# Chunked RWKV attention and a feed-forward layer on one core: `v` cast on GpSimd, joined masks and state sums, a second output bank, and DMA transposes from the 17th chunk on

## The chip, the cores and the metric

The kernel runs on one core of one Trainium2 chip. The time is the device time of one execution in microseconds, and lower is better. The engines carry the profile's names: PE (matrix multiplications; PEld loads its weights), DVE (VectorE), ACT (ScalarE), POOL (GpSimd), SP (SyncE, which issues the DMAs here).

## The reference

The inputs are `r`, `k`, `v`, `w` of shape (4, 8, 768, 48), that is batch, heads, time and head size, `u` of (8, 48), and the weights `w_in` (384, 2048) and `w_out` (2048, 384). In float32:

```python
for t in range(S):
    cur = einsum('bhd,bhe->bhde', u[None] * kt, vt)
    y[:, :, t] = einsum('bhd,bhde->bhe', rt, state + cur)
    state = wt[:, :, :, None] * state + einsum('bhd,bhe->bhde', kt, vt)
x = y.transpose(0, 2, 1, 3).reshape(B * S, H * D)     # 3072 x 384
h = x @ w_in
out = np.maximum(0.01 * h, h) @ w_out                 # 3072 x 384
```

## The kernel before

Time is cut into chunks of 128 steps: 6 chunks for each of the 4 batches, 24 in all, numbered from 0. The state passes from chunk to chunk inside a batch. All matrix products are in bf16.

For one chunk the **attention** goes through these steps (names of tiles as in the profile). Four loads bring `w`, `k`, `r`, `v` into one slot of the ring `in` (11 slots, which the weights use too). ACT takes the logarithm of `w` (`lw`), PE sums it over time (`cp`, with the chunk's total behind it), DVE and ACT make the two exponentials (`ci`, `er`, `ek`), and DVE multiplies them onto `r` and `k` (both halves of `rk`). PE transposes `rk` in eight blocks into a PSUM bank, DVE and ACT copy the halves out (`rkT`). PE makes the scores (banks `se`, `so`: even and odd heads), DVE multiplies them with the mask (`m`, two instructions). `vb` is `v` cast to bf16 (L323, on DVE). PE multiplies the `k` half of `rk` with `vb` (`pp`), DVE adds it to the decayed old state (`s`, two instructions on 64 partitions each), POOL decays the state for the next chunk (`sb`, two instructions, with the factor `a` from ACT). PE adds state and scores up (`yp`), DVE adds the diagonal term that POOL prepared (`ru`, `dg`, `vs`) and gets `y`; PE transposes `y` in three blocks, ACT copies it to `xT`.

The **feed-forward layer** takes each chunk from `xT`: 48 matmuls in four groups of 12 (`hp`, two banks), an activation on ACT after each group (`g`), 16 matmuls in four groups of 4 (`op`, one bank), a copy on DVE (`o`), a store by SP.

PSUM has eight banks: `hp` 2, and one each for `op`, `cp`, `se`, `so`, `yp`, `pp`. The transposes of `rk` go through `se`, those of `y` through `so`.

**What sets the order.** Nothing is recorded in the order of the code. Every step is entered into a `Plan` with an engine, a planned duration, its dependencies and a priority (ten times the chunk number for attention, 1000 and up for the matmuls of the feed-forward layer). The planner goes through time with these planned durations, gives each engine the ready step of the lowest priority number, and adds a delay `LAT` to each result. The order in which it started the steps becomes the order of the instructions of each engine, and on the chip every engine keeps that order and waits where a result isn't there. So a planned duration has no effect on the chip but through the order. Two rules hold the attention near the feed-forward layer: `LEAD` = 4 lets a chunk's logarithm wait for the first `hp` of the chunk four before, and `AHEAD` = 5 lets its loads wait for the `cp` of the chunk five before. `WEIGHTS` says before which chunk's steps, and with which priority, the eight weight loads of 0.79 MB are entered.

Of the kernel before, what the change touches and what calls it, by code (L numbers as in the profile page):

```python
# [8 lines left out]
F32 = mybir.dt.float32  # L9
# [6 lines left out]
class Plan:  # L16
# [3 lines left out]
    LAT = 0.12  # L20
# [15 lines left out]
    def order(self):  # L36
# [18 lines left out]
        while events:  # L55
# [14 lines left out]
            if self.wire[i] is None:  # L70
                done[i] = free[e] + self.LAT
            else:
                dma_free = max(dma_free, free[e]) + self.wire[i]
                done[i] = dma_free + 1.7
# [41 lines left out]
def kernel(  # L116
# [23 lines left out]
    APE = 24  # L140
    NPE = 24
# [3 lines left out]
    WEIGHTS = [(1, 4)] * 4 + [(3, 24)] * 4  # L145
# [6 lines left out]
    def ring(name, count, shape, dtype, where=None):  # L152
        return Ring([(where or pool).tile(shape, dtype, name=f"{name}{i}") for i in range(count)])
# [14 lines left out]
    er_r = ring("er", 3, [128, H, 64], F32)  # L168
# [8 lines left out]
    a_r = ring("a", 3, [128, NP], F32)  # L177
    sx_r = ring("s", 3, [128, NP, D], F32)
# [5 lines left out]
    dram = ctx.enter_context(tc.tile_pool(name="dram", bufs=1, space=bass.MemoryType.DRAM))  # L184
    ad_r = ring("ad", 4, [1, H * 64], F32, dram)
    hp_r = ring("hp", 2, [128, 512], F32, psum)
    op_r = ring("op", 1, [128, DM], F32, psum)
    cp_r = ring("cp", 1, [128, 512], F32, psum)
    se_r = ring("se", 1, [128, NP, 128], F32, psum)
    so_r = ring("so", 1, [128, NP, 128], F32, psum)  # L190
    yp_r = ring("yp", 1, [128, H, D], F32, psum)
    pp_r = ring("pp", 1, [128, NP, 2, D], F32, psum)

    with tc.manual_schedule():
# [3 lines left out]
        for t in sb_r.tiles:  # L198
            nc.gpsimd.memset(t[:], 0.0)
        for t in er_r.tiles:  # L200
            nc.gpsimd.memset(t[:], 1.0)
# [31 lines left out]
        def dve(n, src=60):  # L233
            return (src + n) / 960.0 + 0.03

        def act(n, src=180):
            return (src + n) / 1200.0
# [7 lines left out]
        def weight_steps(q, which, pri):  # L245
# [16 lines left out]
            for half, eng in ((0, "DVE"), (1, "ACT")):  # L262
# [13 lines left out]
                d = dve(384) if eng == "DVE" else act(768, 224)  # L276
# [6 lines left out]
        for n in range(NCH):  # L283
# [19 lines left out]
            if n == 0:  # L303
# [18 lines left out]
                "DVE", dve(DM // 2),  # L322
                lambda vb=vb, vn=vn: nc.vector.tensor_copy(out=vb.t[:], in_=vn.t),  # L323
# [4 lines left out]

            a_pe = n < APE

            def cum(cp=cp, lw=lw, tot=(not first and a_pe)):
# [3 lines left out]
                if tot:  # L335
# [6 lines left out]
            s_cum = step("PE", 0.35 if not first and a_pe else 0.17, cum, P0, reads=[lw], writes=[cp], deps=[s_ln])  # L342
# [12 lines left out]
                    out=er.t[:, :, 0:D], in_=cp.t[:, 0:DM].rearrange("p (h d) -> p h d", h=H), func=AF.Exp),  # L355
                P0, reads=[cp], writes=[er], deps=[s_cum],
# [9 lines left out]
                "DVE", dve(DM),  # L366
                lambda rk=rk, rn=rn, er=er: nc.vector.tensor_tensor(  # L367
                    out=rk.t[:, 0, :, 0:D], in0=rn.t, in1=er.t[:, :, 0:D], op=ALU.mult),
# [3 lines left out]
                "DVE", dve(DM),  # L372
# [6 lines left out]
            if n < NPE:  # L379
                tr = se_r.take()  # L380
                trv = tr.t[:].bitcast(BF16).rearrange("p a (b t) -> p (a b) t", b=2)

                def tpose(rk=rk, trv=trv):
                    for g in range(2 * NP):
                        nc.tensor.transpose(  # L385
                            trv[:, g, :],
                            rk.t[:, g // NP, 2 * (g % NP) : 2 * (g % NP) + 2, :].rearrange("p h d -> p (h d)"),
                            ident[:])
                s_tr = step("PE", 0.6, tpose, P0, reads=[rk], writes=[tr], deps=[s_r, s_k])
                s_t1 = step(  # L390
                    "DVE", dve(512, 120),
                    lambda trv=trv, rkT=rkT: nc.vector.tensor_copy(out=rkT.t[:, 0:NP, :], in_=trv[:, 0:NP, :]),  # L392
                    P0, reads=[tr], writes=[rkT], deps=[s_tr])
                s_t2 = step(
                    "ACT", act(512),
                    lambda trv=trv, rkT=rkT: nc.scalar.copy(out=rkT.t[:, NP:, :], in_=trv[:, NP:, :]),  # L396
                    P0, reads=[tr], writes=[rkT], deps=[s_tr])
                s_T = [s_t1, s_t2]
            else:
# [4 lines left out]
                    P0, reads=[rk], writes=[rkT], deps=[s_r, s_k], wire=1.0)]  # L404
# [13 lines left out]
                "DVE", dve(DM),  # L418
# [3 lines left out]
                "POOL", 1.05,  # L422
# [5 lines left out]
            se, so, yp = se_r.take(), so_r.take(), yp_r.take()  # L428
            sb = None
            if not first:  # L430
                a_in = a_r.take()
                if a_pe:
                    s_adep = step(
                        "ACT", act(NP),
                        lambda a_in=a_in, cp=cp: nc.scalar.activation(  # L435
                            out=a_in.t[:], in_=cp.t[:, DM : DM + NP], func=AF.Exp),
                        P0 + 1, reads=[cp], writes=[a_in], deps=[s_cum])
                else:

                    ad = ad_r.take()  # L440
                    s_row = step(
                        "SP", 0.45,
                        lambda ad=ad, er=er: nc.sync.dma_start(
                            out=ad.t[:], in_=er.t[0:1].rearrange("o h d -> o (h d)")),
                        P0 + 1, reads=[er], writes=[ad], deps=[s_er], wire=0.02)
                    s_sp = step(
                        "SP", 0.45,
                        lambda ad=ad, a_in=a_in: nc.sync.dma_start(
# [236 lines left out]
```

## Time and profile before

| | |
|---|---|
| Time, median of 2 runs | 222.24 us (221.99 to 222.48) |
| The profiled execution | 222.69 us, its span 220.8 us |
| Granted TensorE clock, mean | 0.969 |
| Busy: PE, DVE, ACT, POOL | 186.3, 155.6, 118.7, 98.6 us |
| Moved by DMA | 30.47 MB, 64.7% of 16 engines' span |

The span is what the profile covers; the time of the same execution is 1.9 us longer. A group's row reads: line, engine, operation, output and inputs, shapes, count | busy us in all, mean ns of one | idle time of the engine just before them, and what ended it. In the timeline and in the chain the first number is the start and the second the length, both in us.

### The profile page before, as it was taken

Reading aid. Unit: us, or ns where it says so; the run is one execution under the profiler, and the core shown is the slowest. Engines: PE = TensorE matmul, PEld = TensorE weight load, DVE = VectorE, ACT = ScalarE, POOL = GpSimd, SP = SyncE. Lnnn points to the kernel's source line nnn. Section 1 sums busy time; section 2 is a strip of 40 time slices with the busy share of each in tenths; the row PEclk is TensorE's granted clock in tenths of the full one; section 3 lists DMA queues with packets and bytes.
Section 4 is the critical chain, followed back from the end, with each engine's and each line's share of the span. In section 5 each row is a group of like instructions: output and inputs, shape, how many; then the busy total and the mean of one; then the engine's idle time right before and its main releaser. Section 6 shows DMA issues by size and latency. Waiting matters only on the chain.

```text
span 220.8 us, 6043 instructions
## 1 busy us (share of the span) xinstructions
PE 186.3 (84%) x2448; PEld 144.2 (65%) x2448; DVE 155.6 (70%) x299; ACT 118.7 (54%) x245; POOL 98.6 (45%) x125
## 2 busy tenths in 40 slices
PE   0446679887979998949899999999999999999983
PEld 0246457665667776736686778777777777788861
DVE  6653995589999999996878876977967565620021
ACT  3347367565566655615465547656555655545420
POOL 6312740687663965666787573474412211200000
PEclk9999559999999999988999999999999999999999
DMA  7999999999999999939089267846010110001101
GB/s 130 318 355 184 297 355 165 179 193 189 200 185 216 188 210 201 200 76 181 18 162 177 61 122 147 174 98 128 36 39 2 37 39 36 3 36 39 39 36 71
DMA packets 107179, 30.47 MB, mean 138 GB/s; under 512 B 100368, under 2 KB 105616, under 8 KB 107152
## 3 DMA queue, kind: packets, MB, share of 16 engines
q1 hardware_dynamic: 107152, 30.09, 64.7%
q8 instruction: 19, 0.31, 0.6%
q14 instruction: 8, 0.07, 0.1%
HBM read 25.36 MB, written 4.72 MB: 136 GB/s over the span
## 4 chain that ended last, share of the span: by engine, by line
PE 49%; DVE 23%; DMA 8%; ACT 7%; issue 7%; SPq 2%; POOL 2%; DVEq 0%; ACTq 0%; POOLq 0%
PE hp L579 19%; PE op L631 18%; DVE rk L373 4%; DVE ci L347 3%; DMA in<-in_moe_w_in_dram 3%; DVE m L494 3%; PE se L385 3%; DVE s L510 3%; PE se L471 3%; DMA in<-in_w_dram 2%; DVE y L537 2%; ACT er L354 2%; DMA in<-in_r_dram 2%; DVE vb L323 2%; PE so L547 2%
## 5 line engine op out<-in xcount | busy, mean ns | idle before, releaser
L579 PE MATMUL hp<-xT,w_in_b 128*128 128x128 bf16 x1152 | 81.0, 225 | 0.8 <-ACT xT L553 0.8
L613 ACT ACTIVATE g<-hp 128x512 bf16<-128x512 f32 x96 | 57.4, 598 | 39.4 <-PE hp L579 38.5
L631 PE MATMUL op<-w_out_b,g 128*128 128x384 bf16 x384 | 77.8, 329 | 0.6 <-DVE o L642 0.6
L579 PEld LDWEIGHTS <-w_in_b 128*128 128x128 bf16 x1152 | 72.5, 101 | 7.5 <-issue 1.2
L631 PEld LDWEIGHTS <-g 128*128 128x128 bf16 x384 | 33.1, 98 | 16.5 <-issue 1.8
L462 POOL TENSOR_TENSOR sb<-s,a 64x192 bf16<-64x192 f32 x40 | 25.6, 639 | 28.8 <-ACT a L435 24.9
L411 POOL TENSOR_TENSOR ru<-in,ub 128x384 f32<-128x384 f32 x24 | 24.7, 1033 | 25.0 <-DMA in<-in_r_dram 21.1
L423 POOL TENSOR_TENSOR vs<-in,dg 128x384 f32<-128x384 f32 x24 | 20.0, 834 | 35.2 <-DVE dg L419 11.4
L642 DVE COPY o<-op 128x384 f32<-128x384 f32 x24 | 13.3, 555 | 23.2 <-PE op L631 22.8
L415 POOL TENSOR_TENSOR ru<-ru,in 128x384 f32<-128x384 f32 x24 | 25.7, 1074 | 1.5
L385 PE MATMUL se<-ident,rk 128*128 128x128 bf16 x192 | 18.3, 230 | 7.8 <-DVE rk L367 3.9
L396 ACT COPY rkT<-se 128x512 bf16<-128x512 bf16 x24 | 14.0, 585 | 19.2 <-DVE rkT L392 12.8
L494 DVE TENSOR_TENSOR m<-se,maskb 128x512 bf16<-128x512 f32 x24 | 16.5, 689 | 6.8 <-ACT g L613 3.7
L385 PEld LDWEIGHTS <-rk 128*128 128x128 bf16 x192 | 12.5, 101 | 12.7 <-DVE rk L373 6.0
L367 DVE TENSOR_TENSOR rk<-in,er 128x384 bf16<-128x384 f32 x24 | 18.2, 759 | 2.3 <-ACT er L354 2.1
L347 DVE TENSOR_TENSOR ci<-cp,lw 128x384 f32<-128x384 f32 x24 | 13.3, 553 | 8.3 <-PE cp L337 5.1
L373 DVE TENSOR_TENSOR rk<-in,ek 128x384 bf16<-128x384 f32 x24 | 18.0, 750 | 1.2 <-ACT ek L360 1.1
L537 DVE TENSOR_TENSOR y<-yp,vs 128x384 bf16<-128x384 f32 x24 | 13.2, 550 | 7.8 <-PE yp L526 7.7
L354 ACT ACTIVATE er<-cp 128x384 f32<-128x384 f32 x24 | 11.8, 491 | 10.6 <-DVE ci L347 6.1
L547 PE MATMUL so<-ident,y 128*128 128x128 bf16 x72 | 8.5, 231 | 9.5 <-DVE y L537 9.2
L494 DVE TENSOR_TENSOR m<-so,maskb 128x512 bf16<-128x512 f32 x24 | 16.3, 680 | 0.0
L360 ACT ACTIVATE ek<-ci 128x384 f32<-128x384 f32 x24 | 12.5, 520 | 5.8 <-DVE ci L347 5.8
(42 smaller groups left out, 193.1 us busy)
## 6 DMA issues: line engine op xcount, KB each, us to landing
in<-in_w_dram SPq DMA_DIRECT2D x24, 192.0 KB, 4.2
in<-in_k_dram SPq DMA_DIRECT2D x24, 192.0 KB, 4.1
in<-in_r_dram SPq DMA_DIRECT2D x24, 192.0 KB, 4.4
in<-in_v_dram SPq DMA_DIRECT2D x24, 192.0 KB, 4.4
out_dram<-o SPq DMA_DIRECT2D x24, 192.0 KB, 2.0
in<-in_moe_w_in_dram SPq DMA_DIRECT2D x4, 768.0 KB, 8.2
in<-in_moe_w_out_dram SPq DMA_DIRECT2D x4, 768.0 KB, 8.7
ub<-in_u_dram SPq DMA_DIRECT2D x1, 192.0 KB, 5.0
```

The lines of the kernel that those rows point to most:

```text
L347: lambda cp=cp, ci=ci, lw=lw: nc.vector.tensor_tensor(out=ci.t[:], in0=cp.t[:, 0:DM].rearrange("p (h d) -> p h d", h=H), in1=lw.t[:, :, 0: ...
L367: lambda rk=rk, rn=rn, er=er: nc.vector.tensor_tensor(out=rk.t[:, 0, :, 0:D], in0=rn.t, in1=er.t[:, :, 0:D], op=ALU.mult),
L373: lambda rk=rk, kn=kn, ek=ek: nc.vector.tensor_tensor(out=rk.t[:, 1, :, 0:D], in0=kn.t, in1=ek.t[:], op=ALU.mult),
L385: nc.tensor.transpose(trv[:, g, :], rk.t[:, g // NP, 2 * (g % NP) : 2 * (g % NP) + 2, :].rearrange("p h d -> p (h d)"), ident[:])
L411: lambda ru=ru, rn=rn: nc.gpsimd.tensor_tensor(out=ru.t[:], in0=rn.t, in1=ubv, op=ALU.mult),
L415: lambda ru=ru, kn=kn: nc.gpsimd.tensor_tensor(out=ru.t[:], in0=ru.t[:], in1=kn.t, op=ALU.mult),
L423: lambda vs=vs, vn=vn, dg=dg: nc.gpsimd.tensor_tensor(out=vs.t[:], in0=vn.t, in1=dg.t[:].unsqueeze(2).to_broadcast([128, H, D]), op=ALU.mult),
L462: lambda sb=sb, s_in=s_in, a_in=a_in, q0=q0, half=half: nc.gpsimd.tensor_tensor(out=sb.t[q0 : q0 + 64, :, half, :], in0=s_in.t[q0 : q0 + 6 ...
L494: lambda m=m, sc=sc, par=par: nc.vector.tensor_tensor(out=m.t[:, par, :, :], in0=sc.t[:], in1=maskb[:].unsqueeze(1).to_broadcast([128, NP, ...
L579: nc.tensor.matmul(hp.t[:, a * N : (a + 1) * N], lhsT=w_in_b[:, t, (j + a) * 128 : (j + a + 1) * 128], rhs=xT[:, t, c0 : c0 + N], start=(a ...
L613: lambda hp=hp, g=g, j=j, J=J, N=N: nc.scalar.activation(out=g.t[:, j : j + J, 0:N], in_=hp.t[:, 0 : J * N].rearrange("p (a n) -> p a n", ...
L631: nc.tensor.matmul(op.t[:], lhsT=g.t[:, j, off : off + 128], rhs=w_out_b[:, j, :], start=(j == 0), stop=(j == NJ - 1))
```

## The change

- `v` is cast to bf16 by POOL instead of DVE.
- The scores of even and odd heads share one tile `sc` of two banks, and one mask instruction of 1,024 columns takes the place of two of 512. The transposes of `rk` go through `sc`, in two steps: those of the `r` half no longer stand in one step with those of the `k` half.
- The state is kept with both heads' columns on all 128 partitions; `a` holds zeros where they don't belong together (written by two activations on 64 partitions each). So one state sum on DVE and one decay on POOL take the place of two each.
- `pp`, `yp` and the transposes of `y` share one bank `yp`; the freed bank is a second `op`.
- From chunk 16 on (`NPE` = 16 instead of 24) `rk` and `y` are transposed by one DMA each, issued by SP, with no copy by DVE or ACT.
- The planner's numbers: `LAT` is 0.28 for PE and 0.07 for the others instead of 0.12 for all, many planned durations differ, and `WEIGHTS` enters the loads of `w_in` before chunk 2 with priority 14 (before chunk 1 with 4), those of `w_out` before chunk 4 with 34 (before chunk 3 with 24).

```diff
-    LAT = 0.12
+    LAT = {"PE": 0.28, "DVE": 0.07, "ACT": 0.07, "POOL": 0.07, "SP": 0.07}
...
-    NPE = 24
+    NPE = 16
-    WEIGHTS = [(1, 4)] * 4 + [(3, 24)] * 4
+    WEIGHTS = [(2, 14)] * 4 + [(4, 34)] * 4
...
-    op_r = ring("op", 1, [128, DM], F32, psum)
+    op_r = ring("op", 2, [128, DM], F32, psum)
-    se_r = ring("se", 1, [128, NP, 128], F32, psum)
-    so_r = ring("so", 1, [128, NP, 128], F32, psum)
-    yp_r = ring("yp", 1, [128, H, D], F32, psum)
-    pp_r = ring("pp", 1, [128, NP, 2, D], F32, psum)
+    yp_r = pp_r = ring("yp", 1, [128, 512], F32, psum)
+    sc_r = ring("sc", 1, [128, 2, NP, 128], F32, psum)
...
             s_vb = step(
-                "DVE", dve(DM // 2),
-                lambda vb=vb, vn=vn: nc.vector.tensor_copy(out=vb.t[:], in_=vn.t),
+                "POOL", 0.8,
+                lambda vb=vb, vn=vn: nc.gpsimd.tensor_copy(out=vb.t[:], in_=vn.t),
...
-                    P0, reads=[rk], writes=[rkT], deps=[s_r, s_k], wire=1.0)]
+                    P0, reads=[rk], writes=[rkT], deps=[s_r, s_k], wire=1.75)]
...
-                for half in range(2):
-                    q0 = 64 * half
-                    s_sb.append(step(
-                        "POOL", 0.5,
-                        lambda sb=sb, s_in=s_in, a_in=a_in, q0=q0, half=half: nc.gpsimd.tensor_tensor(
-                            out=sb.t[q0 : q0 + 64, :, half, :], in0=s_in.t[q0 : q0 + 64],
-                            in1=a_in.t[q0 : q0 + 64].unsqueeze(2).to_broadcast([64, NP, D]), op=ALU.mult),
+                s_sb = [step(
+                    "POOL", 1.05,
+                    lambda sb=sb, s_in=s_in, a_in=a_in: nc.gpsimd.tensor_tensor(
+                        out=sb.t[:].rearrange("p g a d -> p (g a) d"),
+                        in0=s_in.t[:].rearrange("p g a d -> p (g a) d"),
+                        in1=a_in.t[:].rearrange("p g a -> p (g a)").unsqueeze(2).to_broadcast([128, H, D]),
+                        op=ALU.mult),
...
-            for par, sc in enumerate((se, so)):
-                s_m.append(step(
-                    "DVE", dve(NP * 128, 120),
+            s_m = [step(
+                "DVE", 1.2,
+                lambda m=m, sc=sc: nc.vector.tensor_tensor(
+                    out=m.t[:].rearrange("p a g t -> p (a g) t"),
+                    in0=sc.t[:].rearrange("p a g t -> p (a g) t"),
+                    in1=maskb[:].unsqueeze(1).to_broadcast([128, H, 128]), op=ALU.mult),
...
+                def state(sx=sx, pp=pp, sb=sb):
...
+                        nc.vector.tensor_tensor(out=sx.t[:], in0=pp.t[:, 0:DM].rearrange("p (g a d) -> p g a d", g=NP, a=2), in1=sb.t[:], op=ALU.add)
...
             if n < NPE:
-                tr = so_r.take()
-                trv = tr.t[:].bitcast(BF16).rearrange("p a (b t) -> p (a b) t", b=2)
+                trv = yp.t[:].bitcast(BF16).rearrange("p (g t) -> p g t", t=128)
```

Three places show what this does to the order. The first is SP's queue in the start, from the last load of chunk 2 (slot `in_75`) on. Before, `w_out` (slots 76 to 79) comes next, then the loads of chunk 4 (slot 70) and chunk 3 (slot 69) in turn:

```order
L297 DMA in_75<-in_v_dram 128x8x48
L255 DMA in_76<-in_moe_w_out_dram 128x4x384
L255 DMA in_77<-in_moe_w_out_dram 128x4x384
L255 DMA in_78<-in_moe_w_out_dram 128x4x384
L255 DMA in_79<-in_moe_w_out_dram 128x4x384
L297 DMA in_70<-in_w_dram 128x8x48
L297 DMA in_70<-in_k_dram 128x8x48
L297 DMA in_69<-in_w_dram 128x8x48
L297 DMA in_69<-in_k_dram 128x8x48
L297 DMA in_69<-in_r_dram 128x8x48
L297 DMA in_69<-in_v_dram 128x8x48
L297 DMA in_70<-in_r_dram 128x8x48
```

And now the same place, where chunk 3 has slot 76, `w_out` has 77 to 79 and 69, and chunk 4 has slot 70:

```order
L290 DMA in_75<-in_v_dram 128x8x48
L290 DMA in_76<-in_w_dram 128x8x48
L290 DMA in_76<-in_k_dram 128x8x48
L290 DMA in_76<-in_r_dram 128x8x48
L290 DMA in_76<-in_v_dram 128x8x48
L248 DMA in_77<-in_moe_w_out_dram 128x4x384
L248 DMA in_78<-in_moe_w_out_dram 128x4x384
L248 DMA in_79<-in_moe_w_out_dram 128x4x384
L248 DMA in_69<-in_moe_w_out_dram 128x4x384
L290 DMA in_70<-in_w_dram 128x8x48
```

Chunk 3's loads moved ahead of `w_out`. In the same way chunk 1's loads now stand ahead of `w_in`, behind which they stood before.

The second place is DVE in the middle, one chunk's round from one `rk` of `k` to the next. Before:

```order
L373 TENSOR_TENSOR rk_91<-in_75,ek_89 128x8x48
L323 CAST vb_101<-in_75 128x384
L419 TENSOR_REDUCE dg_106<-ru_105 128x8
L347 TENSOR_TENSOR ci_83<-cp_146,lw_81 128x384
L537 TENSOR_TENSOR y_125<-yp_149,vs_109 128x384
L392 COPY rkT_95<-se_147 128x512
L510 TENSOR_TENSOR s_121<-pp_150,sb_123 64x192 x2
L367 TENSOR_TENSOR rk_92<-in_76,er_86 128x8x48
L373 TENSOR_TENSOR rk_92<-in_76,ek_88 128x8x48
L323 CAST vb_102<-in_76 128x384
L494 TENSOR_TENSOR m_113<-se_147,maskb 128x512
L642 COPY o_134<-op_145 128x384
```

And now, from one `rk` of `k` to the next:

```order
L366 TENSOR_TENSOR rk_91<-in_75,ek_89 128x8x48
L616 COPY o_134<-op_140 128x384
L512 TENSOR_TENSOR y_125<-yp_142,vs_109 128x384
L387 COPY rkT_95<-sc_143 128x512
L340 TENSOR_TENSOR ci_83<-cp_141,lw_81 128x384
L414 TENSOR_REDUCE dg_108<-ru_105 128x8
L471 TENSOR_TENSOR m_113<-sc_143,maskb 128x1024
L485 TENSOR_TENSOR s_121<-yp_142,sb_123 128x384
L360 TENSOR_TENSOR rk_92<-in_76,er_86 128x8x48
L366 TENSOR_TENSOR rk_92<-in_76,ek_88 128x8x48
```

The cast is gone from DVE's queue, and mask and state sum are one row each.

The third place is SP's queue at the first transposes by DMA, those of `rk` of chunks 16 and 17 (`rkT_94`, `rkT_95`) and of `y` of chunk 16:

```order
L290 DMA in_76<-in_v_dram 128x8x48
L397 DMA_TRANSPOSE rkT_94<-rk_90 128x8x128
L620 DMA out_dram<-o_136 128x384
L290 DMA in_77<-in_w_dram 128x8x48
L290 DMA in_77<-in_k_dram 128x8x48
L290 DMA in_77<-in_r_dram 128x8x48
L290 DMA in_77<-in_v_dram 128x8x48
L397 DMA_TRANSPOSE rkT_95<-rk_91 128x8x128
L620 DMA out_dram<-o_133 128x384
L533 DMA_TRANSPOSE xT<-y_125 128x3x128
L290 DMA in_78<-in_w_dram 128x8x48
```

Before, this queue held loads and outputs alone. The loads of chunks 22 and 23 (slots 77 and 78) and outputs now alternate with the transposes, and each waits for those ahead of it.

More of the change, by code (lines that the diff above doesn't have):

```diff
@@ L371 @@
             s_k = step(
-                "DVE", dve(DM),
+                "DVE", 0.7,
                 lambda rk=rk, kn=kn, ek=ek: nc.vector.tensor_tensor(
@@ L455 @@
+                s_adep = []
+                for half in range(2):
+                    q0 = 64 * half
+                    s_adep.append(step(
+                        "ACT", 0.17,
+                        lambda a_in=a_in, cp=cp, q0=q0, half=half: nc.scalar.activation(
+                            out=a_in.t[q0 : q0 + 64, :, half], in_=cp.t[q0 : q0 + 64, DM : DM + NP], func=AF.Exp),
+                        P0 + 1, reads=[cp], writes=[a_in], deps=[s_cum, s_ci]))
                 s_in, s_sdep = prev
```

161 lines of the change are left out of this document (62 added, 99 removed).

## The prediction

> **What bounds the kernel now.** I began with the page: the span, the busy shares, and the engines in 40 slices of 5.5 us, with what the DMA moved in the fourth row.
>
> ```profile
> span 220.8 us, 6043 instructions
> ...
> PE 186.3 (84%) x2448; PEld 144.2 (65%) x2448; DVE 155.6 (70%) x299; ACT 118.7 (54%) x245; POOL 98.6 (45%) x125
> ...
> PE   0446679887979998949899999999999999999983
> ...
> DVE  6653995589999999996878876977967565620021
> ...
> GB/s 130 318 355 184 297 355 165 179 193 189 200 185 216 188 210 201 200 76 181 18 162 177 61 122 147 174 98 128 36 39 2 37 39 36 3 36 39 39 36 71
> ```
>
> The mean of 84% hides three stages: a start in which PE is half idle, a stretch from the tenth to the eighteenth slice in which DVE stands at 9, and the last half, in which PE does. The busy time by stretches shows the same with numbers (columns: length, PE, PEld, DVE, ACT, POOL busy, then clock, DMA share, GB/s).
>
> ```profile
> 38.00:61.00 23.00, 19.40 (x251) 14.27 (x250) 19.32 (x34) 13.43 (x30) 16.16 (x19) 1.00 1.16 191
> 61.00:98.00 37.00, 31.25 (x455) 24.23 (x453) 36.19 (x67) 21.05 (x46) 24.55 (x29) 1.00 1.01 189
> ...
> 109.00:161.00 52.00, 49.68 (x703) 38.97 (x701) 41.45 (x83) 31.94 (x69) 30.99 (x37) 1.00 0.60 119
> 161.00:184.40 23.40, 22.20 (x315) 17.54 (x314) 15.34 (x30) 13.64 (x31) 4.59 (x7) 1.00 0.08 27
> ```
>
> From 61 to 98 DVE is busy 36.19 of 37 us while PE idles 5.75; after 109 PE is busy 95% and DVE has room. The speed of a stage is the distance between the first up-projections (`hp`) of neighbouring chunks. A chunk has 48 of these matmuls, in chunk order, so the 145th, 193rd, 385th and 769th, and the 961st, open chunks 3, 4, 8, 16 and 20. Their rows in the timeline:
>
> ```profile
> 53.24 0.56 PE L579 MATMUL hp<-xT,w_in_b 128*128 128x128 bf16 x7
> ...
> 60.86 0.55 PE L579 MATMUL hp<-xT,w_in_b 128*128 128x128 bf16 x7
> ...
> 98.44 1.49 PE L579 MATMUL hp<-xT,w_in_b 128*128 128x128 bf16 x12
> ...
> 161.65 1.50 PE L579 MATMUL hp<-xT,w_in_b 128*128 128x128 bf16 x24
> ...
> 192.16 0.84 PE L579 MATMUL hp<-xT,w_in_b 128*128 128x128 bf16 x12
> ```
>
> So chunks 4 to 8 take (98.44 − 60.86)/4 = 9.40 us each, 8 to 16 take 7.90, and 16 to 20 take 7.63. 9.40 is DVE's pace; 7.6 to 7.9 is PE's. The first 61 us yield four chunks.
>
> **The start.** Before, chunk 3's loads stand in SP's queue behind the four loads of `w_out`. The first three rows are from SP's timeline, the last is the first use of chunk 3's `r`.
>
> ```profile
> 21.21 3.21 SPq L255 DMA_DIRECT2D in<-in_moe_w_out_dram  x4
> ...
> 26.63 4.02 SPq L297 DMA_DIRECT2D in<-in_k_dram  x1
> ...
> 35.22 0.84 SPq L297 DMA_DIRECT2D in<-in_r_dram  x1
> ...
> 40.34 1.00 POOL L411 TENSOR_TENSOR ru<-in,ub 128x384 f32<-128x384 f32 x1 [8.43 <-DMA in<-in_r_dram]
> ```
>
> POOL waited 8.43 us, until 40.34, for chunk 3's `r`; chunk 3 reaches PE's `hp` 12.9 us later, at 53.24. Now chunk 3 is issued ahead of `w_out`. In the page's sixth slice the DMAs moved 355 GB/s, so a 0.79 MB weight load is 2.2 us and four are 8.9: chunk 3 lands near 31.5, and `w_out` about 4 us later than before (a chunk's four loads, 0.79 MB at 191 GB/s, are 4.1 us). Chunks 0 to 4 and all weights together are the same bytes and end at the same time, so what is won is order: PE does chunk 3's attention while `w_out` is still under way, instead of after it. I expect chunk 3's `hp` near 45. Chunk 4's loads end near 43 as before, and 10 us from load to `hp` (12.9 for chunk 3, less DVE's relief and queue) gives 53 instead of 60.86: **−8 us**. Ends: nothing, if `w_out`, 4 us later, is what everything waits for; −10, if PE runs without a gap from 45.
>
> **DVE.** What leaves it and what joins, and what POOL takes over, by the groups; the last row is from the line's own view (min/median/max in ns).
>
> ```profile
> L323 DVE CAST vb<-in 128x384 bf16<-128x384 f32 x24 | 14.4, 607 | 0.0
> L494 DVE TENSOR_TENSOR m<-se,maskb 128x512 bf16<-128x512 f32 x24 | 16.5, 689 | 6.8 <-ACT g L613 3.7 <-PE so L471 2.5 <-issue 0.2
> L510 DVE TENSOR_TENSOR s<-pp,sb 64x192 f32<-64x192 f32 x32 | 11.2, 350 | 0.6
> L537 DVE TENSOR_TENSOR y<-yp,vs 128x384 bf16<-128x384 f32 x24 | 13.2, 550 | 7.8 <-PE yp L526 7.7
> L423 POOL TENSOR_TENSOR vs<-in,dg 128x384 f32<-128x384 f32 x24 | 20.0, 834 | 35.2 <-DVE dg L419 11.4 <-DVE y L537 9.0 <-PE cp L337 5.5
> L462 POOL TENSOR_TENSOR sb<-s,a 64x192 bf16<-64x192 f32 x40 | 25.6, 639 | 28.8 <-ACT a L435 24.9 <-ACT er L354 1.5 <-DVE s L510 0.6
> L553 ACT COPY xT<-so 128x384 bf16<-128x384 bf16 x24 | 11.4, 476 | 7.4 <-PE so L547 7.4
> ...
> L367 DVE TENSOR_TENSOR rk<-in,er x24: 541/636/1386, 6.2 to 188.8; 128x384 bf16<-128x384 f32 x24
> ```
>
> The cast takes 0.61 us a chunk with it. The joined mask is one of 1,024 columns: from 384 columns (0.550) to 512 (0.689) is 1.09 ns a column, so 0.689 + 512 × 0.00109 = 1.25 instead of two at about 0.69: 0.13 less. The joined state sum has the shape of `y`, 0.55 instead of 0.70: 0.15 less. Together 0.89 us a chunk. At 9.40 us, where DVE is the pace, that alone gives 8.5; but DVE was also held by waits of its in-order queue (98% busy includes stretched operations), so I take 8.0: 4 × 1.4 = **−5.5 us** for chunks 4 to 8. Ends: 0, and −6.4 at PE's 7.8. On POOL the cast has no row; between 0.34, its least on DVE, and the 1.03 of a two-input `ru` I take 0.8, near the 0.834 of `vs`. The joined `sb` has the shape of `vs`: 0.83 instead of 2 × 0.64. POOL then has about 0.35 us a chunk more, 4.5 of 7.8: hidden. If that cover goes, each 0.1 us a chunk costs 2.4 in all. The second `a` on ACT is small beside ACT's 46% idle.
>
> Against this: `rk` takes 541 ns at best, and up to 1,386, always beside a running POOL operation. The Trainium skill, in "SBUF — State Buffer", section "Who interferes with whom", has it that a DVE instruction with two SBUF inputs and a GpSimd instruction that reads SBUF exclude each other for a whole instruction. The spread of `rk` agrees; by that rule the moved cast would lengthen the two `rk` by some 0.1 us each and give back a fifth of the 0.89.
>
> From chunk 8 to 16 PE sets the pace and nothing leaves it: 0. The shared bank of `pp`, `yp` and the `y` transposes adds a wait: `pp` of a chunk is behind ACT's copy to `xT` of the last, and everything on PE is queued behind `pp`. In the new order 1.1 us or more of other PE work stand between the transposes of `y` and that `pp` in nearly all chunks, against 0.48 for the copy and a place in ACT's queue; I allow **+2 us** in all (0 to +5).
>
> **Chunks 16 to 23.** PE's transposes leave, 8 of `rk` and 3 of `y` a chunk. Rows: the time of four in one run, the time of one, and the DMAs nearest to what replaces them.
>
> ```profile
> 166.41 0.39 PE L385 MATMUL se<-ident,rk 128*128 128x128 bf16 x4
> ...
> L385 PE MATMUL se<-ident,rk x192: 217/220/315, 6.8 to 190.4; 128*128 128x128 bf16 x192
> ...
> in<-in_r_dram SPq DMA_DIRECT2D x24, 192.0 KB, 4.4
> out_dram<-o SPq DMA_DIRECT2D x24, 192.0 KB, 2.0
> ...
> in<-in_moe_w_out_dram SPq DMA_DIRECT2D x4, 768.0 KB, 8.7
> ```
>
> A further transpose in a run costs (0.39 − 0.22)/3 = 0.057 us; eleven are 0.62, eight chunks 5.0. PE is 95% busy there, so I take **−4.5** (0 to −5).
>
> Instead SP issues a transfer of 256 KB for `rk` and one of 96 KB for `y`. None is in the trace. The nearest rows: 192 KB land in 2.0 us (SBUF to HBM, quiet queue) and 4.4 (192-byte pieces, busy queue), 768 KB in 8.7. So `rk` takes 2.7 at the low end (2.0 by bytes), 5.9 to 8.7 at the high; I take 4: SP's queue still holds the last three chunks' loads beside the first three of these transposes, and nothing but outputs beside the other five (DMA share 0.08 after 161). The cover: `rk` is done 2.8 us after `cp` starts, by the chain.
>
> ```profile
> 164.17 0.17 PE cp L332
> ...
> 166.24 0.69 DVE rk L373
> ...
> 210.06 1.34 PE hp L579 x24
> 211.40 2.61 PE op L631 x16
> 214.01 0.02 issue
> 214.03 0.57 DVE o L642
> 214.60 0.04 issue
> 214.64 2.77 PE op L631 x16
> ```
>
> In the new PE order six groups of 12 `hp` (0.67 each, half of 1.34), five of 4 `op` (0.65, a quarter of 2.61) and about 1 us of attention stand between `cp` of chunk 17 and its scores: 8.3 us; counted so, the eight chunks have 7.7 to 10. 2.8 + 4 = 6.8 fits; a landing over 4.9 us begins not to. For `y` the same count gives 9 to 12 us. Queued behind a transpose that waits for `rk` on SP are an output and the transpose of the last `y`; only the four `o` buffers and that `xT` wait for them.
>
> Here the Trainium skill speaks against the change. "VectorE: DVE Perf Modes", section "The three transpose paths", gives 1,309 ns for one 128x128 transpose by DMA and 390 on TensorE; by it, as an estimate, eleven blocks in turn would be 14.4 us a chunk. "Advanced Engine Details and Errata", "X-Bar Transpose (TRN2)", calls these DMAs as fast as ordinary ones. No run here shows either.
>
> **The end.** The last rows above: `op` waits 0.6 us for the copy of `o`; the second bank takes that away: **−0.6**.
>
> Sum: 220.8 − 8 − 5.5 + 2 − 4.5 − 0.6 = 204.2. The profiled execution took 222.69, 1.9 more than its span, and the median of the runs, 222.24, lies 0.45 below it: 205.7, say **206**.
>
> **Rivals.**
> 1. POOL takes back what DVE gives: `rk` at its worst, 1.39 instead of 0.75, twice, is 1.3 us a chunk, more than 0.89. Then chunks 4 to 8 stay at 9.4: 206 + 5.5 and some of the rest, 211 to 214. For it: 24.55 us of POOL in 37 already. Against: the cast itself, stretched to 607 from 344, goes. Chance 0.13.
> 2. The shared bank becomes the loop. With 0.22 for a first matmul and 0.057 for each further one, `pp` is 0.39, `s` 0.55, `yp` 0.85, `y` 0.55, its transposes 0.33, `xT` 0.48, then comes the next `pp`: 3.15 us, plus a place in line at each of five handovers. At 0.93 us each it is 7.8, PE's period; at 1.0 us, 20 chunks lose 0.35 each: 213; at 1.2, 220. For it: the queues of DVE and ACT hold operations of 0.5 to 1.2 us. Against: between 161 and 184 PE was busy 95% with such loops in it. Chance 0.10.
> 3. The transposes land late, 2 to 4 us past their cover. A stall of one chunk's scores also gives the next chunk, whose `cp` is already through, that much more time, so every other chunk stalls: 4 × 2 to 4 = 8 to 16 us, 212 to 222. Chance 0.09.
> 4. Slower: the transposes go block by block and the one queue is their bound. At 2.0 us a block (the `out` row) the eleven take 22 us a chunk, 15 over the 7 that PE needs: 206 + 8 × 15 = 326. It decides from 9.7 us a chunk on, where 8 × 2.7 eat the gain and 2%. For it: nothing in the trace shows a transfer that rearranges two-byte elements. Against: a load of 192 KB, in pieces of 48 floats, goes through in about 1 us. Chance 0.06. By the 14.4 us of the Trainium skill ("VectorE: DVE Perf Modes") it would be 206 + 8 × 7.4 = 265.
>
> **How the numbers follow.** The forecast, 198 to 212, has 0.62. Up to 217 it takes in rival 1, and half of 2 and 3: 0.62 + 0.13 + 0.06 + 0.04, less a few hundredths below 198, is 0.82. So 198 to 217; all the kind ends of the terms at once would give 200 and all the unkind ones 227, and neither meeting is likely. 2% is what a measurement of this kernel tells from no change: faster is under 217.8, slower over 226.7. Faster 0.85, same 0.09, slower 0.06.
>
> **What would show it.** Chunk 4's first `hp` near 53; chunks 4 to 8 at about 8.0 us each; DVE under 90% in that stretch; `vb` on POOL near 0.8 us and `rk` about 0.8; scores of chunks 17 to 23 without a wait on a DMA, transposes landing in about 4 us; 16 to 20 near 7.1. I am wrong if PE waits for `rkT` or `xT`, if `pp` waits for `xT`, or if the first 60 us still yield four chunks.

## The result, and the profile after

The kernel after takes 200.6 us (median of 2 runs, 199.18 to 202.02), 0.9026 of the time before, with a 95% interval of 0.8749 to 0.9304. A longer comparison on another chip gave 199.92 us (199.11 to 200.70) against 224.63, 0.8903 [0.8846, 0.8960]. 206 had been predicted. Ratios are of fast executions alone: one that lies more than 1.5% above its kernel's fastest is left out of them, but not of the medians.

The page of the profiled execution (199.18 us): the span, the busy shares, and the slices, now of 4.9 us, for PE, DVE and the DMA engines.

```profile
span 197.4 us, 5816 instructions
...
PE 175.4 (89%) x2360; PEld 137.7 (70%) x2360; DVE 134.9 (68%) x223; ACT 113.7 (58%) x249; POOL 101.8 (52%) x126
...
PE   0426884999999999999999999999999989999992
...
DVE  6578459856998989699988989647876665441111
...
DMA  6999999989999999989999968989735729422002
```

The stretch in which DVE stood at 9 and PE at 7 to 9 is gone: from the eighth slice on PE stands at 9, with one 8, to the last slice but one, while DVE still stands at 8 or 9 in most slices up to the twenty-fourth. The rows that open chunks 4, 8, 16 and 20, from PE's timeline, and the busy time between them (columns as in the prediction):

```profile
55.19 0.83 PE L553 MATMUL hp<-xT,w_in_b 128*128 128x128 bf16 x12
...
86.07 0.50 PE L553 MATMUL hp<-xT,w_in_b 128*128 128x128 bf16 x6
...
141.67 0.51 PE L553 MATMUL hp<-xT,w_in_b 128*128 128x128 bf16 x6
...
168.57 0.62 PE L553 MATMUL hp<-xT,w_in_b 128*128 128x128 bf16 x8
```

```profile
55.20:86.10 30.90, 30.29 (x446) 24.10 (x445) 26.95 (x43) 19.79 (x47) 27.57 (x33) 1.00 1.06 198
86.10:141.70 55.60, 55.60 (x798) 44.18 (x796) 44.97 (x76) 36.90 (x85) 41.02 (x48) 1.00 0.99 186
141.70:168.60 26.90, 26.01 (x371) 20.49 (x370) 17.76 (x30) 15.62 (x36) 5.42 (x8) 1.00 0.54 85
```

Against the rows of before, the 23.4 us between the two spans (220.8 and 197.4) lie here:

| stretch | before | after | difference | predicted |
|---|---|---|---|---|
| up to chunk 4's first `hp` | 60.86 | 55.19 | −5.7 | −8 |
| chunks 4 to 8 | 9.39 each | 7.72 each | −6.7 | −5.5 |
| chunks 8 to 16 | 7.90 each | 6.95 each | **−7.6** | 0, +2 for the shared bank |
| chunks 16 to 20 | 7.63 each | 6.73 each | −3.6 | −4.5, for chunks 16 to 23 |
| from chunk 20's `hp` to the end | 28.6 | 28.8 | +0.2 | −0.6 |

The largest term is the one that was forecast as nothing. The new operations, by the groups, and the two new transfers from the list of DMA issues (count, median us from issue to landing):

```profile
L471 DVE TENSOR_TENSOR m<-sc,maskb 128x1024 bf16<-128x1024 f32 x24 | 29.2, 1219 | 5.3 <-PE sc L450 4.6 <-ACT ek L353 0.6
...
L316 POOL CAST vb<-in 128x384 bf16<-128x384 f32 x24 | 13.2, 552 | 9.4 <-DMA in<-in_v_dram 7.2 <-PE sc L450 2.2
...
rkT<-rk SPq DMA_TRANSPOSE x8, 3.2
...
xT<-y SPq DMA_TRANSPOSE x8, 2.4
```

### The profile page after: what moved, and what is told of

Same layout as the page of the kernel before. It is cut to its first block, busy times and chain, and to the rows that moved or that the text cites. A ratio compares the mean times of both kernels' runs of the same rounds, so it can differ in the third digit from the quotient of the medians.

```text
span 197.4 us, 5816 instructions
## 1 busy us (share of the span) xinstructions
PE 175.4 (89%) x2360; PEld 137.7 (70%) x2360; DVE 134.9 (68%) x223; ACT 113.7 (58%) x249; POOL 101.8 (52%) x126
## 4 chain that ended last, share of the span: by engine, by line
PE 73%; DMA 8%; DVE 7%; ACT 5%; SPq 2%; issue 2%; POOL 1%; DVEq 0%; POOLq 0%
PE op L605 29%; PE hp L553 29%; PE sc L450 3%; PE sc L379 3%; DMA in<-in_r_dram 3%; DMA rkT<-rk 3%; DMA in<-in_v_dram 2%; PE yp L501 2%; SPq L290 2%; PE yp L461 2%; DVE m L471 2%; PE cp L325 2%; PE yp L497 1%; DVE rk L366 1%; DVE rk L360 1%
## 5 line engine op out<-in xcount | busy, mean ns | idle before, releaser
L605 PEld LDWEIGHTS <-g 128*128 128x128 bf16 x384 | 33.4, 98 | 14.2 <-issue 0.7
L439 POOL TENSOR_TENSOR sb<-s,a 128x384 bf16<-128x384 f32 x20 | 19.6, 978 | 26.1 <-ACT a L432 16.6
L471 DVE TENSOR_TENSOR m<-sc,maskb 128x1024 bf16<-128x1024 f32 x24 | 29.2, 1219 | 5.3 <-PE sc L450 4.6
L366 DVE TENSOR_TENSOR rk<-in,ek 128x384 bf16<-128x384 f32 x24 | 20.5, 853 | 0.9 <-ACT ek L353 0.8
L360 DVE TENSOR_TENSOR rk<-in,er 128x384 bf16<-128x384 f32 x24 | 16.8, 701 | 5.4 <-ACT er L347 5.2
L316 POOL CAST vb<-in 128x384 bf16<-128x384 f32 x24 | 13.2, 552 | 9.4 <-DMA in<-in_v_dram 7.2
L379 PE MATMUL sc<-ident,rk 128*128 128x128 bf16 x128 | 13.2, 235 | 4.8 <-DVE rk L360 2.9
L389 ACT COPY rkT<-sc 128x512 bf16<-128x512 bf16 x16 | 9.4, 586 | 12.7 <-PE sc L379 6.7
L414 DVE TENSOR_REDUCE dg<-ru 128x8 f32<-128x384 f32 x24 | 13.0, 543 | 3.7 <-POOL ru L410 3.6
L379 PEld LDWEIGHTS <-rk 128*128 128x128 bf16 x128 | 8.8, 103 | 7.6 <-DVE rk L360 4.0
L310 ACT ACTIVATE lw<-in 128x384 bf16<-128x384 f32 x24 | 12.5, 520 | 2.1 <-DMA in<-in_w_dram 1.8
```

What stands on the lines that cost most here:

```text
L360: lambda rk=rk, rn=rn, er=er: nc.vector.tensor_tensor(out=rk.t[:, 0, :, 0:D], in0=rn.t, in1=er.t[:], op=ALU.mult),
L366: lambda rk=rk, kn=kn, ek=ek: nc.vector.tensor_tensor(out=rk.t[:, 1, :, 0:D], in0=kn.t, in1=ek.t[:], op=ALU.mult),
L379: nc.tensor.transpose(trv[:, a, g, :], rk.t[:, a, 2 * g : 2 * g + 2, :].rearrange("p h d -> p (h d)"), ident[:])
L439: lambda sb=sb, s_in=s_in, a_in=a_in: nc.gpsimd.tensor_tensor(out=sb.t[:].rearrange("p g a d -> p (g a) d"), in0=s_in.t[:].rearrange("p g ...
L471: lambda m=m, sc=sc: nc.vector.tensor_tensor(out=m.t[:].rearrange("p a g t -> p (a g) t"), in0=sc.t[:].rearrange("p a g t -> p (a g) t"), ...
L605: nc.tensor.matmul(op.t[:], lhsT=g.t[:, j, off : off + 128], rhs=w_out_b[:, j, :], start=(j == 0), stop=(j == NJ - 1))
```

## The experiments

The question was where the 7.6 us between chunks 8 and 16 came from, and whether the gain between 4 and 8 was DVE's relief, as the prediction had it. Three theories: the **order** that the planner's new numbers make (theory 1), the **work** taken from DVE and the new banks (theory 2), the **transposes by DMA** (theory 3). Each run had the kernel before beside it on the same chip (medians 224.59 to 224.81 in the three sets). "Pace" below is the distance of the first `hp` of neighbouring chunks, from one profile of each kernel. Two profiles of the kernel after differ by 0.9 us in chunk 4's `hp` (55.2 and 54.3) and by 0.34 in the pace from 4 to 8 (7.72 and 8.06), so smaller differences in these columns say nothing. A pace also holds the attention that PE does for later chunks in that stretch, and so it moves with where an order puts that work. The last column doesn't: it is the time, in us, in which PE stood idle between the first `hp` of chunks 4 and 20 (1.5 in the kernel after's first profile).

| kernel | time, us | ratio to before, 95% | chunk 4's `hp` | pace 4–8 | 8–16 | 16–20 | PE idle, 4–20 |
|---|---|---|---|---|---|---|---|
| before, first profile | | | 60.9 | 9.39 | 7.90 | 7.63 | 10.5 |
| before, new numbers | 206.15 | 0.9164 [0.9123, 0.9205] | 59.0 | 6.96 | 7.31 | 7.18 | 0.1 |
| before, new latencies only | 218.20 | 0.9716 [0.9659, 0.9774] | 61.7 | 8.44 | 7.78 | 7.52 | 7.0 |
| before, new durations only | 209.22 | 0.9302 [0.9234, 0.9370] | 61.7 | 6.80 | 7.47 | 7.47 | 1.8 |
| before, new numbers and load places | 206.63 | 0.9179 [0.9139, 0.9219] | 60.1 | 6.93 | 7.34 | 7.21 | 0.7 |
| before, `vb` on POOL | 218.22 | 0.9698 [0.9664, 0.9733] | 61.0 | 8.67 | 7.61 | 7.82 | 6.7 |
| before, DMA transposes from chunk 16 | 222.48 | 0.9862 [0.9797, 0.9926] | | | | | |
| after, again | 199.92 | 0.8903 [0.8846, 0.8960] | 54.3 | 8.06 | 6.97 | 6.55 | 2.2 |
| after, old numbers | 214.10 | 0.9535 [0.9450, 0.9619] | 58.9 | 8.94 | 7.48 | 6.95 | 10.9 |
| after, old load places | 203.19 | 0.9037 [0.8970, 0.9104] | 58.7 | 7.52 | 7.28 | 6.50 | 2.8 |
| after, `vb` on DVE | 199.82 | 0.8894 [0.8830, 0.8958] | 55.3 | 7.15 | 7.39 | 6.64 | 3.0 |
| after, all transposes on PE | 206.09 | 0.9184 [0.9097, 0.9271] | 53.6 | 7.96 | 7.56 | 7.34 | 3.8 |
| after, DMA transposes from chunk 8 | 214.12 | 0.9541 [0.9467, 0.9616] | 54.0 | 12.26 | 6.74 | 6.28 | 17.2 |

**The reference**, the kernel after unchanged:

> The kernel after, unchanged, on the chip of this set, so that the other runs have a reference. 198 to 203 us, 0.89 to 0.92 of the kernel before; chunks 4 to 8 at 7.5 to 7.9 us each and 8 to 16 at 6.9 to 7.2.

199.92 us, a ratio of 0.8903, and 6.97 from 8 to 16, as expected; from 4 to 8 the pace was 8.06, above what was expected.

### The order: the planner's numbers alone

The kernel before, with the new numbers, so that the same instructions stand in another order:

```diff
-    LAT = 0.12
+    LAT = {"PE": 0.28, "DVE": 0.07, "ACT": 0.07, "POOL": 0.07, "SP": 0.07}
-                done[i] = dma_free + 1.7
+                done[i] = dma_free + 1.5
-            s_r = step("DVE", dve(DM), ...)        # 0.49; s_k the same
+            s_r = step("DVE", 0.7, ...)
-            s_y = step("PE", 0.45 if sb is None else 0.68, ...)
+            s_y = step("PE", 0.21 if sb is None else 0.38, ...)
-                s_up = step("PE", J * 3 * max(N / 2400 + 0.003, 0.06), ...)
+                s_up = step("PE", J * 3 * (N / 2400 + 0.0025), ...)
...
```

> The kernel before, with only the new numbers of the planner (latencies, DMA latency, durations of the steps that both kernels have); places of the weight loads as before. Theory 1 (the order gives the speed of chunks 8 to 16): these go from 7.90 to 7.1 us each and the time from 222 to 212 to 216. Theory 2 (the work taken from DVE and the banks): 220 to 224, chunks 8 to 16 still at 7.7 to 8.0.

Measured: 206.15 us, 18.7 less than the 224.81 beside it, better than even theory 1 had expected. No operation was taken from any engine (PE has 2,448 matmuls and DVE 299 instructions in both), and the pace from 4 to 8 fell from 9.39 to 6.96. The two windows between the first `hp` of chunks 4 and 20, before and then with the new numbers:

```profile
60.90:192.20 131.30, 120.81 (x1696) 94.23 (x1693) 106.53 (x206) 76.32 (x165) 67.77 (x81) 0.99 0.58 115
```

```profile
59.00:174.00 115.00, 114.89 (x1687) 93.09 (x1684) 102.80 (x206) 77.23 (x164) 67.21 (x83) 1.00 0.71 137
```

The same 206 DVE instructions and nearly the same matmuls take 16.3 us less. PE's idle time falls from 10.5 us to 0.1; the other 5.9 are shorter records of nearly the same work (120.81/1696 = 71.2 ns a matmul, then 68.1). The clock, 0.99 and then 1.00, could account for about 1.2 of these; the rest of that part is open. Between chunks 4 and 8 alone PE is idle 5.9 of 37.5 us before and 0.1 of 27.8 with the new numbers. The other 3.9 us by which that stretch is shorter are PE's own work for later chunks: before, it makes the transposes of six chunks there (66), with the new numbers those of four (44). What PE waited for between chunks 4 and 20 before (first all rows of the matmuls, then the two longest of the weight loads; us in total, times, longest):

```profile
PE so L547 <- DVE y L537: 4.2, 5, 2.6
PE se L471 <- DVE s L510: 1.8, 6, 0.3
PE se L385 <- DVE rk L373: 1.6, 4, 0.6
PE yp L526 <- DVE m L494: 1.3, 5, 0.4
PE pp L482 <- DVE vb L323: 0.5, 1, 0.5
PE se L471 <- DVE s L508: 0.4, 1, 0.4
```

```profile
PEld L547 <- DVE y L537: 6.1, 7, 3.0
PEld L471 <- ACT rkT L396: 4.1, 9, 0.6
```

Every matmul that waited there waited for DVE, and longest for `y`. With the new numbers the same view has no wait of a matmul, and 2.5 us of the weight loads. Why `y` could be late stands in DVE's groups between the first `hp` of chunks 4 and 8, before (60.9 to 98.4) and with the new numbers (59 to 86.8):

```profile
L323 DVE CAST vb<-in 128x384 bf16<-128x384 f32 x9 | 7.1, 807 | 0.0
...
L537 DVE TENSOR_TENSOR y<-yp,vs 128x384 bf16<-128x384 f32 x6 | 3.3, 543 | 0.0
```

```profile
L537 DVE TENSOR_TENSOR y<-yp,vs 128x384 bf16<-128x384 f32 x4 | 2.2, 554 | 1.0 <-PE yp L526 1.0
...
L323 DVE CAST vb<-in 128x384 bf16<-128x384 f32 x4 | 1.4, 350 | 0.0
```

The counts are the point. While PE's feed-forward layer passed four chunks, DVE made nine casts and six `y`: it worked ahead for later chunks, and 98% busy was not the pace of four chunks. The casts cost 807 ns each there and 350 in the other order. The longest wait shows what working ahead can cost, in the rows of DVE and PE before:

```profile
94.34 3.28 DVE L323 CAST vb<-in 128x384 bf16<-128x384 f32 x3
...
97.55 0.55 DVE L537 TENSOR_TENSOR y<-yp,vs 128x384 bf16<-128x384 f32 x1
...
98.15 0.50 PE L547 MATMUL so<-ident,y 128*128 128x128 bf16 x3 [2.62 <-DVE y L537]
```

PE had summed `yp` by 93.7 us, but three casts for later chunks stood ahead of `y` in DVE's queue. PE stood still for 2.62 us. By the count of DVE's rows that `y` is chunk 10's and the casts are those of chunks 12 to 14; chunk 8's first `hp`, which needs none of them, stands behind the transposes of that `y` in PE's queue and starts at 98.44. So a cast that nobody needs yet can delay a `y` that PE waits for, and with it work that needs neither. This accounts for 2.6 of the 10.5 us; how much of the rest the casts ahead cost is not shown.

The latencies and the durations apart: first the latencies alone, which is this part of the edit, and then all the rest of it without this part.

```diff
-    LAT = 0.12
+    LAT = {"PE": 0.28, "DVE": 0.07, "ACT": 0.07, "POOL": 0.07, "SP": 0.07}
-                done[i] = dma_free + 1.7
+                done[i] = dma_free + 1.5
```

> The kernel before with the new latencies of the planner alone (0.28 us behind a PE step, 0.07 behind the others, 1.5 behind a DMA), all durations as before. With all numbers new it took 206.15 us. Theory 1a (PE's 0.28 lets the planner set other work between a PE step and its reader, as the chip needs it): most of the gain is here, 206 to 212, chunks 4 to 8 under 7.8 us each. Theory 1b (the durations do it): 219 to 224, chunks 4 to 8 at 9.0 to 9.4.

> The kernel before with the new durations of the planner alone (a group of hp at 0.67 instead of 0.72 us, rk at 0.7 instead of 0.49, yp at 0.38 instead of 0.68 and so on), latencies as before. Theory 1b (the durations do it: rk and POOL's steps planned near what they take, so that DVE doesn't run ahead with casts of later chunks): 206 to 212, the cast of v under 450 ns in chunks 4 to 8 where before had 807. Theory 1a (the latencies do it): 219 to 224 and the cast at 700 to 800 ns.

218.20 and 209.22 us: 6.4 and 15.4 less than before, where both together gave 18.7. So the durations are the larger part; theory 1a missed, and for the latencies 1b, which gave them nothing, did too. The cast's row between chunks 4 and 8, first with the new latencies, then with the new durations:

```profile
L323 DVE CAST vb<-in 128x384 bf16<-128x384 f32 x8 | 4.9, 619 | 0.0
```

```profile
L323 DVE CAST vb<-in 128x384 bf16<-128x384 f32 x4 | 1.4, 350 | 0.0
```

Where the casts ahead went, the pace came (6.80); where they stayed, it didn't (8.44). They are not the whole of it, though: with the old order and no cast on DVE at all the pace is 8.67, and in the kernel after DVE can make seven casts in this stretch at a pace of 7.15 (both below). So that the planned durations are worth most of the gain is shown, and that the casts ahead are its main part is not. Which of the durations does it was not tried.

The other way round, the kernel after with the old numbers:

> The kernel after, with the planner's numbers of before (latencies, DMA latency, all durations), so that only the order of the instructions changes back; no instruction is added or removed. Theory 1 (the order made by the new numbers gave the 0.95 us a chunk between chunks 8 and 16, and part of 4 to 8): those chunks go back to about 7.9 us each, and the time to 208 to 213 us. Theory 2 (the work taken from DVE and the new banks gave it): within 2 us of the kernel after, 199 to 203, with 6.9 to 7.1 us a chunk from 8 to 16.

214.10, 14.2 more than the kernel after, a little past theory 1. But the loss isn't where it was expected: 3.7 to 4.6 us of it are at the start, 0.9 to 1.2 us a chunk between 4 and 8, and from 8 to 16 0.5 a chunk, 4 us, where all 7.6 had been expected. PE's idle time is that of before again, 10.9 us, with all of the work taken from DVE.

### The work taken from DVE

```diff
-                "POOL", 0.8,
-                lambda vb=vb, vn=vn: nc.gpsimd.tensor_copy(out=vb.t[:], in_=vn.t),
+                "DVE", 0.4,
+                lambda vb=vb, vn=vn: nc.vector.tensor_copy(out=vb.t[:], in_=vn.t),
```

> The kernel after, with the cast of v on DVE again (planned at 0.4 us). Theory 2 (DVE's relief): DVE, busy 26.95 of 30.9 us between chunks 4 and 8, gets 0.61 us a chunk more and loses more to its in-order queue; those four chunks go from 7.7 to 8.3 us each and the next eight from 6.95 to 7.3, so the time is 204 to 207. Theory 1 (the order): DVE has room for it, at most 1 us in all, 200 to 202.

199.82 against 199.92: no difference, theory 1. The move of the cast, taken back, costs nothing in all. The paces moved against each other: from 4 to 8 it is 7.15 instead of 7.72 or 8.06, from 8 to 16 7.39 instead of 6.95 or 6.97. Much of that is only where PE does the attention: 156 of these matmuls instead of 192 fall between 4 and 8, and 302 instead of 282 between 8 and 16. And DVE works ahead here too, in the same stretch from 4 to 8, without a wait of PE for `y`:

```profile
L316 DVE CAST vb<-in 128x384 bf16<-128x384 f32 x7 | 4.2, 593 | 0.0
```

The same move made in the kernel before:

> The kernel before, with the cast of v on POOL (planned at 0.8 us) and nothing else. Theory 2: 0.61 us a chunk leaves DVE; chunks 4 to 8 go from 9.40 to 8.8 us or less, later ones gain little: 218 to 220. If DVE's pace comes from waits and not from its work: 221 to 223. If POOL stretches rk and delays vs: 223 to 226.

218.22, 6.6 less than before, as theory 2 has it. Between the profiles, 2.9 us of it are from 4 to 8 (8.67) and 2.3 from 8 to 16, where theory 2 had little. Both hold: with the old order the move takes the casts ahead out of DVE's queue; with the new order they don't stand in the way. On POOL the cast is not what stretches `rk`. The `k` half of `rk` between chunks 4 and 8, after, and after with the cast on DVE:

```profile
L366 DVE TENSOR_TENSOR rk<-in,ek 128x384 bf16<-128x384 f32 x5 | 5.8, 1158 | 0.0
```

```profile
L366 DVE TENSOR_TENSOR rk<-in,ek 128x384 bf16<-128x384 f32 x4 | 4.4, 1106 | 0.0
```

It is stretched in both; in that stretch it was 908 ns before, and 721 with the new numbers in the kernel before. Over all chunks the two halves of `rk` take 701 and 853 ns after, 759 and 750 before: 0.05 us a chunk more.

The joined operations, the banks and the cast together are told by two kernels with the same numbers and load places, and no transpose by DMA: before with both (206.63, ratio 0.9179) and after with all transposes on PE (206.09, 0.9184). They are equal, so these edits together add nothing to the total that shows. They do shift it: chunk 4's `hp` comes at 53.6 instead of 60.1, and the chunks from 4 to 8, with more of PE's attention in them, then take 7.96 us each instead of 6.93. The second `op` bank and the joins were not tried alone.

### The places of the weight loads

```diff
-    WEIGHTS = [(2, 14)] * 4 + [(4, 34)] * 4
+    WEIGHTS = [(1, 4)] * 4 + [(3, 24)] * 4
```

> The kernel after, with the weight loads where they were before (w_in ahead of chunk 1, w_out ahead of chunk 3). Theory: the load order alone brings chunk 4 forward, so chunk 4's first hp goes from 55.2 back to about 60 and the time to 205 or 206. Rival: the start gains come from DVE's relief and the order, chunk 4's hp stays at 54 to 57 and the time at 199 to 202. Second rival: w_out ahead of chunk 3 is better, since down-projections start earlier (first op at 32 instead of 35): 197 to 199.

203.19, 3.3 more; chunk 4's `hp` at 58.65 instead of 54.3 or 55.2. The first theory's direction, at 0.6 of its size. The new places in the kernel before, beside the new numbers:

> The kernel before, with the new numbers of the planner and the new places of the weight loads, nothing else. If both theories of order hold (numbers and loads), 206 to 210; if the loads alone count, chunk 4's first hp at 55 and 216 to 218; if neither, 220 to 224.

206.63, in the range for both theories, but no better than 206.15 with the numbers alone: there chunk 3's `hp` moves from 51.6 to 44.9, but chunk 4's from 59.0 to 60.1. So the load order pays only with the rest of the kernel after.

### The transposes by DMA

```diff
-    NPE = 16
+    NPE = 24
```

> The kernel after, with all transposes on TensorE in the last eight chunks too (no transpose by DMA). Theory 3, the prediction's term: eleven transposes a chunk at 0.057 us each, eight chunks, 4.5 to 5 us more, 205 to 206, with chunks 16 to 20 at 7.3 us each instead of 6.73. Rival: PE has no slack to give back but the handovers to DVE and ACT come back as well, 7.6 us a chunk, 207 to 209. Rival: the chunks are limited by something else, 200 to 202.

206.09, 6.2 more than 199.92: theory 3, just past its upper end. The pace from 16 to 20 is 7.34, as forecast; but from 8 to 16 it is 7.56 against 6.97, 4.7 us. Part of the reason is in the line's own view of the kernel after (first and last start in us) and in PE's groups between the first `hp` of chunks 8 and 16, before (98.4 to 161.6) and after (86.1 to 141.7):

```profile
L397 SPq DMA_TRANSPOSE rkT<-rk x8: 1232/1241/1854, 122.2 to 168.0; - x8
```

```profile
L385 PE MATMUL se<-ident,rk 128*128 128x128 bf16 x64 | 5.6, 220 | 0.7 <-DVE rk L373 0.4
```

```profile
L379 PE MATMUL sc<-ident,rk 128*128 128x128 bf16 x40 | 3.5, 219 | 0.0
```

Chunk 16's `rk` is transposed at 122.2, 19 us ahead of its `hp`. So while PE passes eight chunks' `hp` it makes the `rk` transposes of five, x40, where before made eight, x64. The gain of chunks 16 to 23 falls largely between chunks 8 and 16. It isn't all PE's own work: with all transposes on PE that stretch has 37 more of them (95 and 58 with those of `y`), about 2.1 us at the prediction's 0.057, and PE is idle 2.0 us in it, where the kernel after has none. In the kernel before:

> The kernel before, with the transposes of the last eight chunks by DMA and nothing else. By the prediction's term 4.5 us less, 217 to 218. If the transposes only matter when the rest of PE's line is tight, 220 to 222.

222.48, a ratio of 0.9862 [0.9797, 0.9926]: by the ratio 3.1 us less, with 1.7 to 4.6 in the interval. That leaves both expectations open; the run doesn't tell whether the transposes are worth less there than in the kernel after.

And eight chunks more, NPE = 8:

> The kernel after, with the transposes by DMA from the 9th chunk on instead of the 17th. If they stay as cheap as late in the kernel, eight chunks win 0.5 to 0.7 us each: 195 to 197, chunks 8 to 16 at 6.4 us. Rival: the loads of later chunks, which fill the DMA queues until 141 us, delay the transposes (landing over 6 us instead of 3.2), PE waits for rkT and xT, and loads stand behind transposes that wait for rk on SP: 201 to 210, chunks 8 to 16 at 7.2 or more.

214.12: the rival's direction, and worse than it said, but not its place. After one stall the paces are the best of all (6.74, where it had 7.2 or more, and 6.28). All is lost at chunk 8, whose `hp` moves from 86.07 to 103.01. From chunk 7's first `hp` (74.7) to chunk 8's, PE is busy half the time:

```profile
74.70:103.00 28.30, 14.49 (x166) 9.97 (x164) 15.09 (x24) 4.88 (x13) 19.74 (x25) 0.68 1.03 204
```

Chunk 8's path, from DVE's and SP's timelines and the chain: its `rk`, its transpose, its `y`, and the transpose of that.

```profile
68.92 1.22 DVE L366 TENSOR_TENSOR rk<-in,ek 128x384 bf16<-128x384 f32 x1
...
88.84 0.56 DVE L512 TENSOR_TENSOR y<-yp,vs 128x384 bf16<-128x384 f32 x1 [0.60 <-PE yp L501]
```

```profile
81.44 0.44 SPq L290 DMA_DIRECT2D in<-in_w_dram  x1
81.98 1.85 SPq L397 DMA_TRANSPOSE rkT<-rk  x1
83.88 0.57 SPq L290 DMA_DIRECT2D in<-in_k_dram  x1
...
98.29 1.66 SPq L397 DMA_TRANSPOSE rkT<-rk  x1
100.04 0.53 SPq L620 DMA_DIRECT2D out_dram<-o  x1
100.66 3.80 SPq L533 DMA_TRANSPOSE xT<-y  x3
```

`rk` was done at 70.1 and its transpose was issued 11.8 us later, behind the loads of later chunks; `y` was done at 89.4 and its transpose issued 11.3 us later, behind loads and the `rk` transposes of chunks 10 and 11. The transfers themselves landed in 3.7 and 3.1 us (medians), not in the 6 that the rival had. The wait is in SP's queue, not in the transpose. None of these kernels is faster than the kernel after by more than the measurement. Taken back one at a time, the numbers cost 14.2 us, the transposes 6.2, the load places 3.3 and the cast nothing: 23.7 of the 24.7 us.

## Why the prediction was right, and where not

The sign and the range held; the sum did so partly through terms whose reasons fell. That is in part luck: the order alone, for which the sum has no term, is worth more than any term in it, and its terms for DVE and for the weights' places, 13.5 us together, stood in for it.

- **Start, −8: −5.7.** The load places account for 3.5 to 4.4 us in the kernel after (58.65 against 55.2 and 54.3). The mechanism held there, with chunk 3's `hp` at 46.7 (45 forecast) and `w_out` later as forecast (first `op` at 35.1 us instead of 31.9), and the size was off. In the kernel before, with the new numbers, the same places gave nothing.
- **Chunks 4 to 8, −5.5 from DVE's relief: −6.7, but not from that.** The failed step is "9.40 is DVE's pace", and with it the price of DVE's relief. A window's length over the chunks that PE passed was divided without a count of what DVE did in it: nine casts, six `y`. The order alone takes PE's idle time between chunks 4 and 20 from 10.5 us to 0.1; all the rest of the change, with the old numbers, leaves it at 10.9. POOL, forecast at 4.5 of 7.8, was busy 27.57 of 30.9 us there; PE stood idle for only 0.6 of them. The prices of the single operations were near: joined mask 1.25 forecast and 1.219 measured, `vb` on POOL 0.8 and 0.552.
- **Chunks 8 to 16, "nothing leaves it: 0", +2 for the shared bank: −7.6.** This term was mis-sized. "7.6 to 7.9 is PE's" took 95% busy for PE's pace. Of the 7.6, 4.7 to 4.9 are the transposes by DMA, which the prediction booked from chunk 16 on although attention runs ahead, and the other 2.7 are what the kernel after with all transposes on PE has below before (7.90 to 7.56). That 7.90 was not PE's least, the kernel before itself shows: with the new numbers it does these chunks in 7.31. No wait on the shared bank showed: PE was busy 55.60 of 55.60 us.
- **Transposes, −4.5: −6.2 in all.** The landing, forecast at 4 us for `rk`, was 3.2, and 2.4 for `y`. In the last 56 us PE waited for them 0.9 us, once. Rival 3 did not come at NPE = 16; it did at NPE = 8, from SP's queue. Rival 4 was not near: the eight blocks land together in 3.2 us. The 1,309 ns a block of the Trainium skill ("VectorE: DVE Perf Modes", "The three transpose paths") would be, as an estimate, 10.5 us for them, and the measurement decides against it in this form. The Trainium skill's "Advanced Engine Details and Errata", "X-Bar Transpose (TRN2)", which has them as fast as ordinary DMAs, agrees in order of size: the 192 KB of `out` landed in 2.0 us before.
- **The end, −0.6: nothing.** The wait of `op` for `o` went (0.6 us before, none after), but the stretch from chunk 20 took 28.8 instead of 28.6.
- **What was missing** is a term for the order itself. The prediction described the planner's numbers, priced only the weights' places among them, and left out what, alone, is 18.7 us where the whole change is 24.7. Rival 1 did not come: the `k` half of `rk` went to 1,158 ns between chunks 4 and 8, but it was 908 before and with the cast on DVE 1,106, and over all chunks `rk` cost 0.05 us a chunk more, where rival 1 needed 1.3.
- **Two slips in the working** change nothing above: 4 × 1.4 is 5.6, and rival 2's five handovers at 1.2 us give 233, not 220.

## What to carry to other kernels

Before a stage's length is called an engine's pace, count in that window how often the engine ran each operation: more than one a chunk means that it works ahead, and an order that holds this work back can be worth more than taking the work away. In a kernel whose order is planned, the planned durations and delays are worth tuning like any other part; here changing them removed no work and won 8%. A transfer that replaces PE work pays from where its chunk's preparation runs, and only while the issuing queue is free; look at what stands ahead of it there.

## What the runs showed of the hardware

A DMA transpose of 128 x 1,024 bf16 elements (256 KB) landed in 3.2 us, of 128 x 384 (96 KB) in 2.4, and SP was held about 1.2 us by each issue in the kernel after; with NPE = 8, among the loads, an issue for `rk` held it 1.66 us (medians). A POOL cast of 128 x 384 from float32 to bf16 took 0.55 us on average; on DVE, between chunks 4 and 8, it took 0.35 in the order with the new numbers and 0.81 in that of before. Where PE sat idle half the time in the kernel with NPE = 8, its granted clock fell to 0.68 for that stretch.
